# A transformer block written as one list of steps: the first loads, the order of the steps, and one core of a Trainium2

## The chip, the cores and the metric

One NeuronCore of one Trainium2 chip runs the kernel. The metric is device time in microseconds (us). The engines named here are TensorE (PE; its weight loads have a row of their own, PEld), VectorE (DVE), ScalarE (ACT), GpSimd (POOL) and SyncE (SP). DMAs are issued from SP and from ACT; in the profile such a row carries the name of the issuing queue, SPq or ACTq.

## The reference

```
x = A_x                                    # 2048 rows of 448, bf16
xn = layernorm(x)
q, k, v = split(xn @ wqkv)                 # 16 heads of 28
phi(a) = [softmax(a @ w_phi), softmax(-a @ w_phi)]      # per head, over 28 features
kv = phi(k)^T v ; z = sum of phi(k)
o = phi(q) kv / (phi(q) z + 1e-6)
out = x + o @ wo + mish(xn @ w1 + b1) @ w2               # w1 448 x 1792, w2 1792 x 448
```

## The kernel before

The 2048 rows are 16 tiles of 128 rows (t = 0 to 15), taken in 8 pairs (u = t // 2). For each tile the mean and the variance are found (on DVE, or on ACT in three steps at lines 493 to 497), then the reciprocal root (on ACT at lines 513 and 515, or on POOL at lines 508 and 510), then the normalised rows `xn`. Each pair is turned on its side into `xnT`, by TensorE with a copy behind it (pairs 0 and 1), or by a DMA that transposes (the others, line 551). Each row pair has 448 = 3 x 128 + 64 columns, so each product with a weight runs in three parts: A and B are the 128-row chunks, in two halves of the array that work side by side, and H is the last 64 rows.

The weights of the feature maps are folded: `Wpk` is the key weight times `w_phi`. TensorE first turns the key weights (`w_tr`, line 583; half 0 needs only the main part, rows 0 to 383, and half 1 needs the tail too, rows 384 to 447), then multiplies by `w_phi` (`w_mm`, line 613). The query weights come already turned, by four DMA transposes `lqT0` to `lqT3` (line 307); a copy on DVE (`qd`, line 311) doubles their last columns, and `w_mm` makes `Wpq`. Then come the products of keys, values and queries (line 464, `k`, `v`, `q`), exponentials on ACT (lines 720 and 793), the sums on DVE and the scaling of the keys on POOL (lines 728 to 744, `kn` and `kc`), the first matmul of the feed-forward part with its Mish on ACT (`f`, lines 464 and 814), `kv` (line 761), the attention (`nd`, line 834), its output projection (`wo`, line 956) and the second matmul of the feed-forward part (`g`, line 939), and the stores.

Every step is a small function that has a short name. A string `ORDER` lists the names, and `run_order` calls them one after the other, so each engine gets its instructions in the order of that list. Nothing else decides the order: semaphores are put in where a step reads what another engine or a DMA wrote. The names that matter here: `lx a.b` loads x tiles a to b-1, from SP (`s`) or ACT (`a`); `lkm` and `lvm` load the main part of the key and of the value weights, `lkt` and `lvt` their tails; `st` finds mean and variance, `rt` and `rs` the reciprocal root, `xn` normalises, `xt` turns a pair; `wtk0`, `wtk1` turn the key weights, `wmk` and `wmq` multiply by `w_phi`; `z` and `y` are matmuls on zeros that only keep TensorE running (line 405).

The tail of the key weights is one DMA of 64 rows by 896 columns, which also holds the tail of the value weights for the lower half of the array; the second tail load brings the value weights for the upper half:

```
def load_kv_tail(i, eng):
    lo, hi = HALF[i]
    dst, src = (Wv, A_wqkv[384:448, 2 * D:3 * D]) if i else (Wkv, A_wqkv[384:448, D:3 * D])
    dma(eng, lambda e: e.dma_start(dst[lo:hi, 3, :], src), w=[("Wt", i)], tag=f"ldWt{i}")
...
r = [("Wk", 0)] + ([("Wt", 0)] if h else []) + [("ident",)]          # w_tr: what half h reads
```

Of the kernel before, what the change touches and what calls it, by code (L numbers as in the profile page):

```python
# [144 lines left out]


ORDER = """
zero pw pp table lx0.2a lkma lx2.4s lkta lvta lbs st2d st1d lx4.6a pi st3a z11 st0d lps rt1a lvms rt3a rt2p xn1a xn2d
rt0p xn3d lx10.12s b1 xn0d wtk0b wtk1b xt1a lx8.10a xt0d lqT3 wmk0a st4d lqT2 st5d wmk1a v1Ba rt4p lqT1 xn4p lqT0 v0Ba
l1c0a v1Aa lx6.8s lx12.14s l1c1s v0Ha st10d v1Ha rt5p qd v0Aa st11d k1A k1H wmq1a st9d rt10p rt9p wmq0a rt11p k0B k1B  # L150
xn5d st8d k0A rt8p st7d xn10d q0A st12d xn11d xn8p xt2m k0H st6d st13d q0H xn9d q1B lx14.16s rs3p xn7d q0B xn6d q1A
rt12p st15d rt13p k2A xn12d xt5m k2H xn13d v2Ad q1H k2B q2B st14d xt4m v2Bd q2A k5A xt3m v2Hd rs7p xt6m q2H xn15p k5B
v5Ba k5H v4Aa v5Ha v4Ha xn14a kn2.0 k4H kn0.0 kc5 kn2.1 k4A v4Ba v5Aa k4B e2 k3B e3 xt7m v6Hd l1c2s v6Ad k3H q4H k3A
l1ts v6Bd e0 q4B kn0.1 k6B kn4.1 kn4.0 q4A pv k6H v7Bd k7H k6A k7B v7Hd los f0.8B v7Ad ep k7A f0.8H f0.6B f0.4B e5
f0.6A f0.8A f0.6H v3Ba f0.4A e8 v3Ha f0.7B v3Aa f0.1A kn1.0 f0.4H f0.7A f0.7H kc6 kn7.1 e1 f0.1H kn7.0 f0.3B f0.1B q7B
f0.3H kn1.1 f0.3A q5H kn3.1 e4 q3B q5B q3H e9 q3A q5A f1.4B kn3.0 q7H q7A f1.4A l2p1s kv0 kv7 e11 kv4 kv6 kv5 pk kv2
kv3 kv1 e14 f1.12B kvz f1.3B e10 f1.12A f1.4H wob f1.3A f1.3H f0.12B f1.12H f1.9A f1.9H f0.5H f0.5A f1.9B f0.0H f0.5B
f0.0B nd1 f0.0A f0.9A e15 f0.12H f0.9H f0.12A nd0 f0.10A e6 f0.9B f1.10B f0.10H f1.6A f1.6H nd2 l2p0a f0.10B f1.6B
l2p3s ot0m f1.10A f1.10H f1.1H f1.11B f1.1A f1.11H nd4 f1.1B f1.7B f1.11A e7 f1.8H nd3 f1.7A f1.8B f1.0H f1.0A ot1m
f1.7H f0.13H f0.13A f1.0B f1.5H f0.13B f1.8A f1.5B nd6 f0.2B f1.5A f0.2H f1.2H f0.2A f1.2A nd5 f1.13H f1.2B f1.13B  # L160
f0.11A l2p2a f0.11H nd7 q6A f1.13A q6H f0.11B ot2m q6B wo0H ot3m wo0A nd11 nd10 wo0B e12 g1 g7 e13 ot5m g0 wo3A nd12
nd13 wo2A wo2H wo3B ot6m wo2B nd14 wo3H g6 g5 g11 g4 g10 nd15 wo5B wo6A ot7m nd9 wo5A sto2 wo5H nd8 wo6B g12 g2 g8 g3
g14 ot4m wo1H wo4B wo1B wo7B wo4A wo1A wo6H wo4H wo7H wo7A sto0 g13 g9 sto1 stt14 g15 sto6 sto5 y0.1 sto3 sto4 y3.4
stt15
"""


# [942 lines left out]
```

## Time and profile before

| | |
|---|---|
| median of 3 runs | 155.65 us (150.18 to 155.79) |
| the profiled execution's own time | 150.82 us |
| its span in the trace | 149.0 us |
| PE busy | 145.1 us, 97% of the span |
| DVE, ACT, POOL busy | 99.3, 76.3, 43.2 us |
| DMA moved | 17.17 MB |

Times in the trace count from the span's start. A row gives start, duration, engine, line, operation, output <- input and how many instructions are merged in it; in square brackets stands how long the engine was idle before it and what ended that. A busy TensorE is not one at its peak, since matmuls overlap: the distance between starts tells more.

### The profile page before, as it was taken

The page shows a single profiled execution, that of the slowest core. Times are in us where ns is not written, and L with a number is a line of the kernel's source. Part 1 is how long each engine was busy: PE and PEld are TensorE (multiplying, and loading weights), DVE is VectorE, ACT ScalarE, POOL GpSimd, SP SyncE. Part 2 cuts the span into 40 slices and gives each one's busy share as a digit, 9 for nine tenths or more (in the row PEclk, how much of TensorE's full clock was granted, in tenths as well). Part 3 has the DMA queues.
Part 4 walks back from the last instruction along what each step waited for, and adds up shares of the span by engine and source line. Part 5 has one row for each costly group of instructions (what it writes and reads, how often), then busy time and mean ns, then how long its engine had stood idle before and what let it go on. Part 6 is the DMA issues. An engine that isn't in the chain of part 4 may idle for free.

```text
span 149.0 us, 3632 instructions
## 1 busy us (share of the span) xinstructions
PE 145.1 (97%) x1544; PEld 75.2 (50%) x1545; DVE 99.3 (67%) x222; ACT 76.3 (51%) x91; POOL 43.2 (29%) x66
## 2 busy tenths in 40 slices
PE   7897999999999999999999999999999999999996
PEld 2464544555444484454444545545555555547453
DVE  0885999999999303089794799588993399301722
ACT  3895999998988995774757839400000000000000
POOL 5425683999999992000000000000000000000000
DMA  4999459999997038974702133943030023220252
GB/s 121 320 249 317 106 132 164 157 239 218 212 224 183 4 57 107 191 168 122 133 4 40 26 92 66 109 93 62 7 62 0 0 41 87 56 67 4 92 185 92
DMA packets 40372, 17.17 MB, mean 115 GB/s; under 512 B 34084, under 2 KB 39844, under 8 KB 40356
## 3 DMA queue, kind: packets, MB, share of 16 engines
q1 hardware_dynamic: 38148, 14.37, 48.4%
q10 hardware_dynamic: 2208, 2.56, 5.8%
q8 instruction: 12, 0.20, 0.6%
q14 instruction: 4, 0.03, 0.1%
HBM read 6.97 MB, written 1.84 MB: 59 GB/s over the span
## 4 chain that ended last, share of the span: by engine, by line
PE 90%; SPq 5%; DMA 3%; issue 0%; DVE 0%
PE PS L464 48%; PE PS L939 28%; PE PS L956 7%; DMA WqT<-in_A_wqkv_dram 3%; SPq L307 2%; PE PS L834 2%; PE PS L761 2%; SPq L330 1%; PE PS L405 1%; PE PS L613 1%; SPq L287 1%; SPq L334 0%; SPq L290 0%; PE PS L921 0%; DVE WqT L311 0%
## 5 line engine op out<-in xcount | busy, mean ns | idle before, releaser
L464 PE MATMUL PS<-xnT,W 64*128 64x512 bf16 x392 | 45.3, 376 | 0.0
L939 PE MATMUL PS<-W,actT 128*128 128x448 bf16 (+1 forms) x224 | 42.7, 351 | 0.0
L814 ACT ACTIVATE actT<-PS,b1T 128x1024 bf16<-128x1024 f32 x28 | 30.1, 1112 | 12.2 <-PE PS L464 12.2
L939 PEld LDWEIGHTS PS<-W,actT 128*128 128x128 bf16 x224 | 21.6, 98 | 20.7 <-issue 1.3
L464 PEld LDWEIGHTS PS<-xnT,W 64*128 64x128 bf16 x392 | 18.1, 94 | 21.3 <-ACT actT L814 0.8
L904 DVE TENSOR_TENSOR x_all<-PS,x_all 128x448 bf16<-128x448 f32 (+1 forms) x16 | 9.3, 615 | 17.0 <-PE PS L956 9.2
L732 POOL TENSOR_TENSOR actT<-actT,rSk 128x896 bf16<-128x896 bf16 x12 | 20.0, 1697 | 0.0
L720 ACT ACTIVATE actT<-PS 128x896 bf16<-128x896 f32 x16 | 14.2, 1034 | 0.7 <-PE PS L464 0.7
L464 PE MATMUL PS<-Wpk,xnT 64*128 64x448 bf16 x112 | 13.2, 349 | 0.0
L464 PE MATMUL PS<-Wkv,xnT 64*128 64x448 bf16 x112 | 13.1, 349 | 0.1
L464 PE MATMUL PS<-Wpq,xnT 64*128 64x448 bf16 x112 | 13.0, 349 | 0.0
L728 DVE TENSOR_REDUCE Sk<-actT 128x32 f32<-128x896 bf16 x12 | 12.5, 1040 | 0.0
L849 DVE COPY Sq<-PS 128x16 f32<-128x16 f32 x32 | 4.0, 168 | 12.1 <-PE PS L834 12.1
L501 DVE BATCH_NORM_STATS2 stats<-x_all 128x6 f32<-128x448 bf16 x15 | 9.2, 610 | 4.1 <-DMA x_all<-in_A_x_dram 4.1
L860 DVE TENSOR_TENSOR xn<-v_all,rden 128x448 bf16<-128x448 f32 x16 | 10.0, 624 | 2.2 <-DMA Wkv<-xn 1.7
L857 DVE TENSOR_TENSOR v_all<-v_all 128x464 f32<-128x464 f32 x16 | 10.3, 643 | 0.6
L853 DVE TENSOR_TENSOR v_all<-PS,Sq 128x464 f32<-128x464 f32 x16 | 10.3, 641 | 0.5
L855 DVE TENSOR_TENSOR v_all<-PS,Sq 128x464 f32<-128x464 f32 x16 | 10.1, 630 | 0.0
L793 ACT ACTIVATE actT<-PS 128x896 bf16<-128x896 f32 x10 | 8.8, 987 | 0.3 <-PE PS L464 0.3
L464 PEld LDWEIGHTS PS<-Wkv,xnT 64*128 64x128 bf16 x112 | 5.3, 94 | 5.5 <-ACT actT L720 0.3
L464 PEld LDWEIGHTS PS<-Wpq,xnT 64*128 64x128 bf16 x112 | 5.3, 94 | 5.3 <-ACT Eq L793 0.3
L464 PEld LDWEIGHTS PS<-Wpk,xnT 64*128 64x128 bf16 x112 | 5.4, 94 | 5.1 <-ACT actT L793 0.4
(84 smaller groups left out, 135.5 us busy)
## 6 DMA issues: line engine op xcount, KB each, us to landing
out_dram<-x_all SPq DMA_DIRECT2D x7, 224.0 KB, 2.2
W<-in_B_w_dram SPq DMA_DIRECT2D x3, 448.0 KB, 4.9
x_all<-in_A_x_dram SPq DMA_DIRECT2D x5, 224.0 KB, 4.4
W<-in_B_w_dram ACTq DMA_DIRECT2D x2, 448.0 KB, 3.8
x_all<-in_A_x_dram ACTq DMA_DIRECT2D x3, 224.0 KB, 3.8
Wo<-in_A_wo_dram SPq DMA_DIRECT2D x2, 336.0 KB, 5.3
W<-in_B_w_dram SPq DMA_DIRECT2D x2, 224.0 KB, 4.9
Wkv<-in_A_wqkv_dram ACTq DMA_DIRECT2D x1, 336.0 KB, 4.4
```

Source lines behind the costliest of these rows:

```text
L464: ins = e.matmul(o, lhs(c, k), rhs(c, k), start=first and n == at[par][0], stop=last and n == at[par][-1])
L720: op("ACT", lambda e, s=s: e.activation(E_of(u)[:, s, :, :], two(b, D), ACT.Exp, scale=1.0 if s == 0 else -1.0), r=[pb(b), pb(b + 1)], w=[ ...
L728: op("DVE", lambda e: e.tensor_reduce(Sk[u][:, s, :], Eh(), AX.X, ALU.add), r=[("E", u, s)], w=[("Sk", u, s)], tag=f"Sk{u}.{s}")
L732: op("POOL", lambda e: e.tensor_tensor(Eh(), Eh(), ap_on(rSk[u][:, s, 0:1], [[1, 2 * H], [0, DH]]), ALU.mult), r=[("E", u, s), ("rSk", u, ...
L814: op("ACT", lambda e: e.activation(actT[:, q, fc, :], bank(b, 2), ACT.Mish, bias=b1T[:, fc:fc + 1]), r=[("b1T",), pb(b), pb(b + 1)], w=[(" ...
L853: op("DVE", lambda e: e.tensor_tensor(tv(t1[i]), num(0), sx(1), ALU.mult), r=[pb(b), pb(b + 1), ("Sq", i, 1)], w=[("t1", i)], tag=f"ta{t}")
L855: op("DVE", lambda e: e.tensor_tensor(tv(t2), num(1), sx(0), ALU.mult), r=[pb(b), pb(b + 1), ("Sq", i, 0)], w=[("t2",)], tag=f"tb{t}")
L857: op("DVE", lambda e: e.tensor_tensor(t1[i], t1[i], t2, ALU.add), r=[("t1", i), ("t2",)], w=[("t1", i)], tag=f"tc{t}")
L860: op("DVE", lambda e: e.tensor_tensor(o_sb[(t // 2) % 2][:, t % 2, :].rearrange("p (h d) -> p h d", d=DH), t1[i][:, :, 0:DH], ap_on(rden[i ...
L904: op("DVE", lambda e: e.tensor_tensor(x_all[:, t, 0:n], bank(b)[:, 0:n], x_all[:, t, 0:n], ALU.add), r=[pb(b), ("x", t)], w=[("out", t)], ...
L939: ins = e.matmul(bank(b)[:, 0:width(t)], act_of(fc, t), W2[:, fc, 0:width(t)], start=first and fc == 0, stop=last and fc == FC - 1)
L956: ins = e.matmul(bank(b)[:, 0:w], oT_of(u)[lo:hi, cc * P:(cc + 1) * P], Wo[lo:hi, cc, 0:w], start=first and n == at[par][0], stop=last and ...
```

## The change

Only the list `ORDER` changes; no step's function does. What the words for it mean in the list: the first x loads become `lx1.2s`, `lx2.4a`, `lx0.1a` (tile 1 alone from SP, tiles 2 and 3 from ACT, tile 0 alone from ACT) in place of `lx0.2a` and `lx2.4s`; the key weights' main part comes from SP (`lkms`) and both tails follow on ACT, behind ACT's statistics of tile 3 (`lkta`) and behind the reciprocal root of tile 2 (`lvta`); the third part of W2 (`l2p2a`) is loaded early; the values of pair 1 begin with part H; and the rest of the list stands in another order, with another choice of engine for some copies, roots and normalisations.

```
-zero pw pp table lx0.2a lkma lx2.4s lkta lvta lbs st2d st1d lx4.6a pi st3a z11 st0d lps rt1a lvms rt3a rt2p xn1a xn2d
-rt0p xn3d lx10.12s b1 xn0d wtk0b wtk1b xt1a lx8.10a xt0d lqT3 wmk0a st4d lqT2 st5d wmk1a v1Ba rt4p lqT1 xn4p lqT0 v0Ba
-l1c0a v1Aa lx6.8s lx12.14s l1c1s v0Ha st10d v1Ha rt5p qd v0Aa st11d k1A k1H wmq1a st9d rt10p rt9p wmq0a rt11p k0B k1B
...
-g14 ot4m wo1H wo4B wo1B wo7B wo4A wo1A wo6H wo4H wo7H wo7A sto0 g13 g9 sto1 stt14 g15 sto6 sto5 y0.1 sto3 sto4 y3.4
-stt15
+lx1.2s zero st1d lx2.4a pi pw lbs st2d lx0.1a table lkms st0d st3a lkta y0.1 rt1p rt2a lvta xn1d y1.2 z7 lps xn2d rt3a
+rt0a lx8.12s lvms lx4.6s b1 xn3d lqT0 xn0d lqT3 wtk0b wtk1b xt1a st10d lqT2 xt0b wmk0a st11d lqT1 wmk1a st9d lx6.8s pp
+rs5a v1Ha st5d v1Aa v0Ba st4d l2p2a qd v1Ba rs2p v0Aa st8d v0Ha lx12.14a rt9a rt8p k1H k0H xn5d xn4d xn11d k1A l1c1s
+xn8d st6d xn10d rt6p wmq1a wmq0a k0B k1B xn9p lx14.16s st7d q0H st14d k0A st12d q1H st15d rt7p q0B q1B xt2m xt5m q0A
...
+g3 g9 ot4m sto0 wo4B wo7B wo6H wo6A wo1B wo4H wo4A wo1A wo1H wo7A wo7H wo6B sto5 g8 g13 sto2 g12 sto1 sto4 g14 sto6
+g15 stt14 stt15
```

On ACT, at the program's start, before the change: all of its first five DMAs stand ahead of the first statistics (line 493, tile 3). Line 287 loads x, line 290 the main part of the key weights, line 304 the two tails.

```order
L351 ACT_TABLE_LOAD
L287 DMA x_all<-in_A_x_dram 128x896
L290 DMA Wkv<-in_A_wqkv_dram 128x3x448
L304 DMA Wkv<-in_A_wqkv_dram 64x896
L304 DMA Wkv<-in_A_wqkv_dram 64x448
L287 DMA x_all<-in_A_x_dram 128x896
L493 ACTIVATE junk1,mv<-x_all 128x448 [waits dma_0]
```

And with the change, at the same place on ACT (dma_58 is the load of tiles 2 and 3):

```order
L287 DMA x_all<-in_A_x_dram 128x896
L287 DMA x_all<-in_A_x_dram 128x448
L351 ACT_TABLE_LOAD
L493 ACTIVATE junk1,mv<-x_all 128x448 [waits dma_58]
L495 ACTIVATE rmean<-mv 128x1 [waits done_ACT]
L497 ACTIVATE junk1,mv<-x_all,rmean 128x448 [waits done_ACT]
L304 DMA Wkv<-in_A_wqkv_dram 64x896
L513 ACTIVATE lnv<-mv,eps_col 128x1 [waits done_POOL,done_DVE]
L515 ACTIVATE rstd<-lnv 128x1 [waits done_ACT]
L304 DMA Wkv<-in_A_wqkv_dram 64x448
```

The two tails (line 304) moved behind three and behind five instructions of ACT that each have a wait, and the main part of the key weights left this queue.

On SP, at the start, before the change; line 334 loads b1, line 330 the four pieces of `w_phi`, line 290 the main part of the value weights, line 307 the transposes of the query weights:

```order
L287 DMA x_all<-in_A_x_dram 128x896
L334 DMA b1_rows<-in_B_b1_dram 14x128
L330 DMA Wbd<-in_A_w_phi_dram 28x4x28 [waits done_POOL]
L330 DMA Wbd<-in_A_w_phi_dram 28x4x28 x3
L290 DMA Wkv<-in_A_wqkv_dram 128x3x448
L287 DMA x_all<-in_A_x_dram 128x896
L307 DMA_TRANSPOSE WqT<-in_A_wqkv_dram 128x448 x4
```

And with the change; the first line 290 is now the key weights, the second the value weights:

```order
L287 DMA x_all<-in_A_x_dram 128x448
L334 DMA b1_rows<-in_B_b1_dram 14x128
L290 DMA Wkv<-in_A_wqkv_dram 128x3x448
L330 DMA Wbd<-in_A_w_phi_dram 28x4x28 [waits done_POOL]
L330 DMA Wbd<-in_A_w_phi_dram 28x4x28 x3
L287 DMA x_all<-in_A_x_dram 128x1792
L290 DMA Wkv<-in_A_wqkv_dram 128x3x448
L287 DMA x_all<-in_A_x_dram 128x896
L307 DMA_TRANSPOSE WqT<-in_A_wqkv_dram 128x448 x4
```

The four transposes of the query weights moved behind two more issues.

On PE, the first products behind the zero matmuls, with the change (dma_2 is the main part of the key weights, dma_60 the first tail, dma_61 the second); before the change the same rows stand there in the same order up to the first line 464, with 11 zero matmuls in place of 10:

```order
L405 MATMUL PS<-zeros 128x512 [waits done_POOL]
L405 MATMUL PS<-zeros 128x512 x9
L806 MATMUL PS<-ident,b1_rows 128x14 [waits dma_1,done_POOL]
L583 MATMUL PS<-ident,Wkv 112x128 [waits dma_2]
L583 MATMUL PS<-ident,Wkv 112x128 x7
L583 MATMUL PS<-ident,Wkv 112x128 [waits dma_60]
L583 MATMUL PS<-ident,Wkv 112x128 x3
L583 MATMUL PS<-ident,Wkv 112x64 x4
L539 MATMUL PS<-ident,xn1 128x128 [waits done_DVE]
L539 MATMUL PS<-ident,xn1 128x128 x6
L539 MATMUL PS<-ident,xn0 128x128 [waits done_DVE]
```

Nothing moved here: the second half of the key weights' turn (the row that waits dma_60) still stands ahead of the turn of the first rows (line 539) and of all that follows.

More of the change, by code (lines that the diff above doesn't have):

```diff
@@ L147 @@
 ORDER = """
-zero pw pp table lx0.2a lkma lx2.4s lkta lvta lbs st2d st1d lx4.6a pi st3a z11 st0d lps rt1a lvms rt3a rt2p xn1a xn2d
-rt0p xn3d lx10.12s b1 xn0d wtk0b wtk1b xt1a lx8.10a xt0d lqT3 wmk0a st4d lqT2 st5d wmk1a v1Ba rt4p lqT1 xn4p lqT0 v0Ba
-l1c0a v1Aa lx6.8s lx12.14s l1c1s v0Ha st10d v1Ha rt5p qd v0Aa st11d k1A k1H wmq1a st9d rt10p rt9p wmq0a rt11p k0B k1B
-xn5d st8d k0A rt8p st7d xn10d q0A st12d xn11d xn8p xt2m k0H st6d st13d q0H xn9d q1B lx14.16s rs3p xn7d q0B xn6d q1A
-rt12p st15d rt13p k2A xn12d xt5m k2H xn13d v2Ad q1H k2B q2B st14d xt4m v2Bd q2A k5A xt3m v2Hd rs7p xt6m q2H xn15p k5B
@@ L153 @@
[L153 to L162, printed above, removed]
@@ new lines @@
+xn6d q1A v2Bd k2A v2Hd xt4m st13d pv rt14a rt12p l1c0a xn7d v2Ad k2H k5B rt13p rt15p k2B xn13d k5A v5Ad pk xt3m k5H
+xn12d k4H k4A xn14p v5Bd xt6m v4Ha e2 k4B v4Aa e3 kn2.1 xn15p kn1.1 v5Hd q2B v4Ba q2H q2A k3B q4B v6Bd xt7m l1c2a
+kn4.0 k3A kn4.1 e4 v6Hd l1ta k6A kn1.0 k3H k6H v6Ad q4H k6B q4A v3Bd k7A k7H kn2.0 kn3.0 v3Ad v3Hd e9 e0 k7B f0.4B
+f0.3A f0.4H e5 v7Ha e1 f0.3B f0.4A kc0 f0.1B v7Ba f0.3H f0.7B f0.1A f0.1H loa e8 f0.8A f0.7H f0.7A f0.8B v7Aa q3A
+l2p1a f0.6B q3H f0.8H kn7.1 f0.6A ep f0.6H f1.4A q3B q7B q5A l2p0s kn6.0 kn6.1 kn3.1 f1.4B q5B q7A q7H q5H kv1 kv2 kv4
@@ new lines @@
+kv6 kv3 kc5 kv5 kv0 kn7.0 kv7 e15 kvz f1.4H f1.3H f1.1B f1.3A f1.11A e10 f1.1H f1.11H e14 f1.3B f1.9B f1.11B f1.9A
+f1.9H f0.5H f1.1A f0.10A f0.10H f1.0A f1.0H nd3 l2p3a f0.10B f0.5A f1.0B f0.5B nd0 f1.6B f1.12H f1.12A f1.2H f1.6H
+f1.6A f1.2B f1.12B nd1 f0.2B f1.2A e7 f0.2A f1.5H f0.2H f1.7A nd2 f1.7H f1.5B e11 f0.13H f1.7B f0.13A ot0m f1.5A nd4
+e6 ot1m f1.8B f0.13B f1.8H f1.8A f0.9A nd6 f1.13B f1.10H f0.9H f1.13H f1.13A f1.10B nd7 f1.10A f0.11B f0.9B f0.0B
+f0.11H nd5 f0.11A f0.12B f0.0A f0.12A f0.0H q6A f0.12H ot3m q6H ot2m wo0B nd11 wo0A q6B e12 wo0H nd10 g0 g1 g6 e13
@@ L165 @@
+nd13 wob ot5m wo3A wo3H nd12 ot6m wo3B nd14 g11 g7 g10 nd8 wo2B wo5H wo5A wo2A sto3 nd15 wo2H nd9 wo5B ot7m g4 g5 g2
+g3 g9 ot4m sto0 wo4B wo7B wo6H wo6A wo1B wo4H wo4A wo1A wo1H wo7A wo7H wo6B sto5 g8 g13 sto2 g12 sto1 sto4 g14 sto6
+g15 stt14 stt15
 """
```

## The prediction

> **What bounds the kernel now.** I read the page's busy table first, then the chain that ended last, then the timeline of its start.
>
> ```profile
> PE 145.1 (97%) x1544; PEld 75.2 (50%) x1545; DVE 99.3 (67%) x222; ACT 76.3 (51%) x91; POOL 43.2 (29%) x66
> ```
>
> ```profile
> 8.56 5.07 DMA WqT<-in_A_wqkv_dram
> ...
> 13.65 0.24 DVE WqT L311
> ...
> 13.94 0.96 PE PS L613 x16
> 14.90 37.59 PE PS L464 x382
> 52.49 3.27 PE PS L761 x128
> ...
> 146.11 0.41 PE PS L921 x14
> ```
>
> From 14.90 us to 146.52 us the chain is TensorE alone, 131.6 us without a break. The work in that stretch is the same before and after. 382 matmuls in 37.59 us are 0.098 us each. So the time is the moment at which this dense stretch begins, plus what TensorE must still do, plus a tail of 149.0 - 146.5 = 2.5 us for the last addition and store, which the change leaves (tile 15 is still last and still split). The zero matmuls that stood at the very end run beside that store and give nothing back.
>
> What ends last ahead of the stretch is the DMA transpose of the query weights, which lands at 13.63; the product that reads it starts at 13.94. What TensorE does earlier is in the timeline:
>
> ```profile
> 0.96 4.68 PE L405 MATMUL PS<-zeros 128*128 128x512 bf16 x11 [0.96 <-POOL zeros L357]
> 1.28 0.46 ACTq L290 DMA_DIRECT2D Wkv<-in_A_wqkv_dram  x1
> 1.78 1.17 ACTq L304 DMA_DIRECT2D Wkv<-in_A_wqkv_dram  x2
> 4.13 0.58 ACT L493 ACTIVATE junk<-x_all 128x448 bf16<-128x448 bf16 x1 [2.03 <-DMA x_all<-in_A_x_dram]
> 5.07 0.67 ACT L497 ACTIVATE junk<-x_all,rmean 128x448 bf16<-128x448 bf16 x1
> 5.71 1.31 PE L583 MATMUL PS<-ident,Wkv 128*112 128x128 bf16 x16
> 7.43 1.22 PE L539 MATMUL PS<-ident,xn 128*128 128x128 bf16 x14 [0.42 <-DVE xn L527]
> 8.04 0.33 ACTq L287 DMA_DIRECT2D x_all<-in_A_x_dram  x1
> 8.06 0.58 ACT L544 ACTIVATE Eq<-PS 112x512 bf16<-112x512 bf16 x1
> 8.54 0.91 ACT L544 ACTIVATE xnT<-PS 128x896 bf16<-128x896 bf16 x1
> 9.51 2.82 PE L464 MATMUL PS<-Wkv,xnT 64*128 64x448 bf16 x28
> 12.16 0.92 PE L464 MATMUL PS<-Wpk,xnT 64*128 64x448 bf16 x8
> 13.94 0.96 PE L613 MATMUL PS<-Wbd,WqT 112*128 112x112 bf16 x16 [0.85 <-DVE WqT L311]
> ```
>
> The last row is the only wait of any size behind 9.51: 0.85 us. The gain that a better start could bring is therefore small: this wait, and some of the gaps ahead of 9.51.
>
> **The change, part by part.** The first load's size. Tiles 2 and 3 go out first on ACT, at about 0.85 us, and ACT's statistics of tile 3 (4.13 above, behind a load of the same size issued at 0.81) stay where they were, at 4.15. Tile 1 alone is half the bytes; its saving is bounded by the store rows:
>
> ```profile
> out_dram<-x_all SPq DMA_DIRECT2D x7, 224.0 KB, 2.2
> out_dram<-x_all SPq DMA_DIRECT2D x1, 112.0 KB, 1.7
> Wkv<-in_A_wqkv_dram ACTq DMA_DIRECT2D x1, 336.0 KB, 4.4
> Wkv<-in_A_wqkv_dram SPq DMA_DIRECT2D x1, 336.0 KB, 4.7
> Wkv<-in_A_wqkv_dram ACTq DMA_DIRECT2D x1, 112.0 KB, 4.4
> ```
>
> At most 0.5 us earlier for `xn1`, which nothing can use while TensorE waits for weights. I take 0.
>
> The key weights' main part. It moves from 1.28 on ACT to 1.27 + 0.44 + 0.05 = 1.76 on SP; with 4.4 us to landing it is there at 6.16 and not at 5.68. TensorE turns its first half at 6.2, half a microsecond late. What hides this is the next part.
>
> The tails. This is the term that I expect to decide. A DMA on ACT's queue is issued when the waits of the instructions ahead of it are met, not when ACT has run them: the row of 8.04 goes out before the copies of 8.06 and 8.54 that stand ahead of it have started. By the order, the first tail now stands behind the three steps of tile 3's statistics; the wait of the last (the row of 5.07) is met at about 5.06. So the tail is issued at **5.1 us** and not at 1.78. Queued behind it on ACT is nothing that another engine waits for sooner. Its time to landing: 4.4 us by its own row, where it stood behind 560 KB on the same queue; the x loads go from 2.7 to 5.0:
>
> ```profile
> DMA to landing us min/median/max: 2.7/3.9/5.0
> ```
>
> I take the median, 3.9, since its queue is now empty but SP's holds 784 KB: it lands at **9.0 us** (7.8 to 10.1). TensorE takes its instructions in order, and the second half of the key weights' turn stands ahead of everything else. So TensorE is idle from about 6.7 to 9.0.
>
> From there to the values: eight transposes 0.45 us, seven of pair 1 0.4 us, 0.2 us until the last has landed; beside it ACT copies the turned weights (0.58 us, the row of 8.06, done at 10.2), then the turned pair 1 (0.91 us), and the values start at 9.0 + 2.2 = **11.2** against 9.51. The second tail goes out behind tile 2's root, at 6.15 (that row stood at 6.13 before), and lands by 10.6 with the 4.4 us: in time. Then 28 + 10 matmuls of 0.098 us, as the order has two more key products ahead of the query weights: TensorE is at the query weights' product at 11.2 + 3.72 = **14.9** (13.7 to 16.0 with the landing).
>
> The query weights. These rows give what the transposes stand behind on SP:
>
> ```profile
> 0.81 0.40 SPq L287 DMA_DIRECT2D x_all<-in_A_x_dram  x1
> 1.27 0.44 SPq L334 DMA_DIRECT2D b_rows<-in_B_b_dram  x1
> 1.76 1.92 SPq L330 DMA_DIRECT2D Wbd<-in_A_w_phi_dram  x4
> 3.73 0.42 SPq L290 DMA_DIRECT2D Wkv<-in_A_wqkv_dram  x1
> 4.19 0.48 SPq L287 DMA_DIRECT2D x_all<-in_A_x_dram  x1
> 4.71 5.12 SPq L307 DMA_TRANSPOSE WqT<-in_A_wqkv_dram  x4
> ```
>
> Two more issues, 0.46 and 0.52 us, put the first at 5.69 and the fourth at 9.54. With the 5.07 us of the chain it lands at 14.61; the copy (0.24) and 0.05 + 0.05 us put the product at **14.95**. With the shortest of the four times to landing, 4.1, it would be 14.0. Both paths meet at 14.95, which is 1.01 later than 13.94, with two more matmuls (0.2 us) done: **+0.8 us**. The third part of W2, issued on ACT behind ACT's next wait (11 us or later), shares the DMA engines with the last transpose; that is within the 5.07, which had a 448 KB load of W1 beside it.
>
> The new order of the rest. TensorE has 131.6 us of work either way; its cover is that each next operand is there. The nearest thing to a limit is POOL, which scales the keys:
>
> ```profile
> 26.15 1.04 POOL L533 TENSOR_SCALAR xn<-x_all,rstd,shift 128x64 bf16<-128x64 bf16 x2 [0.94 <-DMA xnT<-xn]
> 27.16 3.35 POOL L732 TENSOR_TENSOR actT<-actT,rSk 128x896 bf16<-128x896 bf16 x2
> 46.31 8.32 POOL L732 TENSOR_TENSOR actT<-actT,rSk 128x896 bf16<-128x896 bf16 x5
> ```
>
> Before, the last scaling ends at 54.6, 0.3 us ahead of the `kv` that reads it (seventh of eight, 52.49 + 6 x 0.41 = 54.95). Now tile 14 is normalised on POOL too (0.7 us), and waits as tile 15 did for the transpose of pair 3; with that landing at about 27.1, 1 us later than before, 16 scalings of 1.67 us and the two normalisations end at 55.6, and the last `kv` stands at 53.3 + 7 x 0.41 = 56.2. Slack 0.6 us: I take 0. The far ends: +1.4, that transpose 2 us later still; and -1.4, the two longest waits of TensorE's weight loads in the stretch all gone, though matmuls ran beside them, so that little of it is there to gain:
>
> ```profile
> PEld PS L464 <- ACT actT L814: 0.8, 3, 0.3
> PEld PS L464 <- DVE v_all L855: 0.6, 2, 0.3
> ```
>
> Sum against the profiled execution: 150.82 + 0.8 = **151.6 us**. That execution is 0.64 us above the lowest run shown, 150.18, and 4.83 below the median, 155.65, a level of which this trace shows nothing. From 2% a measurement of this kernel tells a change from none: below 147.8 or above 153.8 by the profiled execution.
>
> **The rivals.**
>
> The tail is no wait: were it issued early or landed by 8 us, the landing of the query weights alone would set the product, at 14.0 to 14.9, less the 0.2. Time 150.7 to 151.6, or 149.3 with the whole -1.4. For it speaks the emptier queue; against it that the issue needs the wait of the row of 5.07.
>
> TensorE's rate falls back. The zero matmuls at the start take 4.68 / 11 = 0.43 us each for 512 columns, where this stretch at the end has four in 1.04:
>
> ```profile
> 146.57 1.04 PE L405 MATMUL PS<-zeros 128*128 128x512 bf16 x4
> ```
>
> So TensorE starts at half its rate and has the full one only after 4.3 to 4.8 us of running. With the change the zero matmuls end at 0.96 + 10 x 0.43 = 5.2, and until 9.0 only one group of eight transposes (0.45 us) runs. If this gap takes the rate back, the next 4.3 us of running, from 9.0 on, count half: +2.15 us, 153.8; if twice as long, +4.3, 155.9. It decides from the point where the gap is long enough, and ends on the slow side. For it: 3.4 us idle of 3.8. Against it: nothing in this trace shows a fall. The Trainium skill, "TensorE: Matmul & The Clock Gate", in "What's actually happening", has the clock halved after a free-running window of about 3.4 us without activity, and restored after a busy one; by that rule the gap is about as long as one window, so it would hit some executions and spare others. No run here shows it yet.
>
> The feed. POOL's scalings or the late transposes come 1 to 2 us later than I have them: the `kv` products wait, 152.6 to 153.6. For it: slack of 0.6 us. Against: pairs 2 to 6 are turned, by the same hand count, about 1 us before TensorE reads them.
>
> The two levels. If what lifts two of the three runs to 155.7 lies in this start, the change may end it or fix it: 151.6 would then stand 2.6% under 155.65, or 155.65 + 0.8 = 156.5 over it. Nothing speaks for either.
>
> **How the numbers follow.** Forecast 151.6 (own range 150.8 to 152.6): 0.47. Tail no wait: 0.17. Rate falls back: 0.17. Feed: 0.07. Levels: 0.12, mostly upward in time. The range leaves out the far ends of the first two rivals and takes in the levels: 149.8 to 156.9. Faster by over 2% comes only from the levels, 0.10, as no sum from the rows reaches 147.8. Slower by over 2%: the rate's fall, and a little of the feed and the levels, 0.20. Within 2%: 0.70.
>
> **What would show it.** Right: a line 493 of ACT at 4.1, the first line 304 on ACTq at 5.1, the second eight of line 583 on PE behind an idle time of over 2 us that ends at about 9.0, the values (line 464) from 11.2, the product of the query weights (line 613) from about 15, and from there about 131.4 us to the last line 921. Wrong: an idle time under 0.5 us ahead of the second half of line 583 (tail no wait); 28 value matmuls in 5 us and not 2.8 (rate); idle POOL ahead of line 732 and idle PE ahead of line 761 (feed).

## Result, and the profile after

The changed kernel takes 160.83 us (median of 6 runs, 159.4 to 161.27). Against the kernel before, timed on the same chip, the ratio is **1.067, 95% interval 1.058 to 1.076**: slower by 6 to 8%. The forecast was 151.6 us, with a range up to 156.9. The profiled execution takes 160.7 us with a span of 159.0 us, 10.0 us longer than before. (The kernel before reads 150.0 to 150.7 us as a median on the chips of the experiments; runs more than 1.5% above the fastest of their kernel are left out of all ratios.)

On the page after, the row of TensorE's busy share (40 slices of 4.0 us) has a hole in the second and third slice and another in the eleventh; the row of the granted clock (PEclk, in tenths) shows 5 in the third and fourth, and 8 and 7 in the eleventh and twelfth:

```profile
PE   7539999999399999999999999999999999999993
...
PEclk9955999999879999999999999999999999999999
```

The timeline of the start, with the rows that answer to those of the prediction:

```profile
4.77 0.53 ACTq L304 DMA_DIRECT2D Wkv<-in_A_wqkv_dram  x1
...
5.72 0.65 PE L583 MATMUL PS<-ident,Wkv 128*112 128x128 bf16 x8 [0.29 <-DMA Wkv<-in_A_wqkv_dram]
...
10.60 1.18 PE L583 MATMUL PS<-ident,Wkv 128*112 128x128 bf16 x8 [4.23 <-DMA Wkv<-in_A_wqkv_dram]
...
14.82 3.05 PE L464 MATMUL PS<-Wkv,xnT 64*128 64x448 bf16 x28
...
18.75 0.96 PE L613 MATMUL PS<-Wbd,WqT 112*128 112x112 bf16 x16
```

The tail goes out at 4.77 as foreseen, TensorE is idle for 4.23 us until it has landed, and the product of the query weights starts at 18.75 and not at 13.94. From there to the end of the last line 921 are 137.8 us (156.53), where it was 132.6 before; behind it both kernels have 2.5 us. So of the 10.0 us the **start has 4.8** and the **dense stretch 5.2**. Where the stretch loses is seen in the list of TensorE's waits, and in the chain:

```profile
PE PS L583 <- DMA Wkv<-in_A_wqkv_dram: 4.5, 2, 4.2
PE PS L464 <- DMA xnT<-xn: 2.7, 1, 2.7
```

```profile
4.77 5.79 DMA Wkv<-in_A_wqkv_dram
...
34.32 7.83 DMA xnT<-xn
...
42.29 12.19 PE PS L464 x98
```

The second wait is for the DMA transpose of pair 7, which takes 7.83 us. What stands on the queues around it, after, and then around the same transpose before (the row at 28.47):

```profile
33.78 0.34 ACTq L294 DMA_DIRECT2D W<-in_B_w_dram  x1
34.16 0.47 ACTq L298 DMA_DIRECT2D W<-in_B_w_dram  x1
34.32 1.31 SPq L551 DMA_TRANSPOSE xnT<-xn  x1
35.01 0.48 ACTq L298 DMA_DIRECT2D W<-in_B_w_dram  x1
```

```profile
28.47 1.26 SPq L551 DMA_TRANSPOSE xnT<-xn  x1
29.78 0.69 SPq L294 DMA_DIRECT2D W<-in_B_w_dram  x1
30.51 1.19 SPq L298 DMA_DIRECT2D W<-in_B_w_dram  x2
```

Before, the third block of W1 and its last rows (448 and twice 224 KB) stand on SP, behind the transpose, which took 3.3 us. After, they are issued from ACT, two of them just ahead of the transpose and one 0.7 us behind it.

The third cost is the clock. Busy time, granted clock and DMA share of core 0 in stretches, after:

```profile
8.00:9.00 1.00, 0.00 (x0) 0.74 1.00 281
9.00:12.00 3.00, 1.40 (x11) 0.50 1.37 150
12.00:15.00 3.00, 3.00 (x32) 0.50 0.93 245
15.00:16.00 1.00, 1.00 (x10) 0.84 0.73 283
...
42.00:43.00 1.00, 0.71 (x6) 0.81 0.22 45
43.00:46.00 3.00, 3.00 (x18) 0.50 0.95 178
46.00:47.00 1.00, 1.00 (x12) 0.98 2.48 133
```

The means of the mixed rows give the edges (a mean of 0.74 over 8 to 9 is full clock up to 8.48 and half behind it): at half from about 8.5 to 15.3, and again from about 42.6 to 46.0. The first fall comes in the middle of the wait, the second when work has been going for 0.3 us already. These lengths are twice 3.4 us and once 3.4 us, and the 27.3 us from the end of the one to the start of the other are eight times 3.4: the edges lie on one grid. One such window at half takes 0.5 x 3.41 / 155 = 0.011 off the mean clock of an execution, so the mean clock counts them: this one has 0.967, three windows, and all six executions have 0.967 or 0.968.

The Trainium skill, "TensorE: Matmul & The Clock Gate", section "What's actually happening", gives a free-running window of 3413 ns; the lengths here agree.

### The profile page after: what moved, and what is told of

It is laid out like the page before. It is cut to its first block, busy times and chain, and to the rows that moved or that the text cites. A ratio compares the mean times of both kernels' runs of the same rounds, so it can differ in the third digit from the quotient of the medians.

```text
span 159.0 us, 3626 instructions
## 1 busy us (share of the span) xinstructions
PE 148.2 (93%) x1539; PEld 79.9 (50%) x1539; DVE 100.3 (63%) x223; ACT 76.8 (48%) x96; POOL 40.5 (25%) x59
## 4 chain that ended last, share of the span: by engine, by line
PE 76%; DMA 10%; ACT 8%; POOL 2%; DVE 1%; issue 1%; ACTq 0%
PE PS L464 35%; PE PS L939 27%; PE PS L956 7%; DMA xnT<-xn 5%; DMA Wkv<-in_A_wqkv_dram 4%; ACT actT L720 3%; PE PS L834 2%; PE PS L761 2%; DMA x_all<-in_A_x_dram 2%; PE PS L613 1%; ACT Wpq L544 1%; POOL actT L732 1%; ACT actT L793 1%; ACT Eq L793 1%; PE PS L539 1%; PE PS L583 1%
## 5 line engine op out<-in xcount | busy, mean ns | idle before, releaser
L464 PEld LDWEIGHTS PS<-xnT,W 64*128 64x128 bf16 x392 | 19.6, 94 | 20.6 <-issue 2.0
L464 PE MATMUL PS<-Wpk,xnT 64*128 64x448 bf16 x112 | 13.8, 370 | 2.7 <-DMA xnT<-xn 2.7
L720 ACT ACTIVATE actT<-PS 128x896 bf16<-128x896 f32 x16 | 13.4, 939 | 5.9 <-DVE v_all L546 4.4
L464 PE MATMUL PS<-Wkv,xnT 64*128 64x448 bf16 x112 | 14.3, 371 | 0.0
L464 PEld LDWEIGHTS PS<-Wkv,xnT 64*128 64x128 bf16 x112 | 5.9, 99 | 6.1 <-issue 1.2
L793 ACT ACTIVATE actT<-PS 128x896 bf16<-128x896 f32 x10 | 8.7, 968 | 0.0
```

Source lines behind the costliest of these rows:

```text
L464: ins = e.matmul(o, lhs(c, k), rhs(c, k), start=first and n == at[par][0], stop=last and n == at[par][-1])
L720: op("ACT", lambda e, s=s: e.activation(E_of(u)[:, s, :, :], two(b, D), ACT.Exp, scale=1.0 if s == 0 else -1.0), r=[pb(b), pb(b + 1)], w=[ ...
L793: op("ACT", lambda e, s=s: e.activation(Eq_of(u)[:, :, s, :].rearrange("p i (h n) -> p i h n", n=64)[:, :, :, 0:QP], two(b, D).rearrange(" ...
```

## Experiments

The theory formed from the two traces has three mechanisms: the late tail with the clock that falls in its wait, the transpose slowed by W1's loads, and small things in the rest of the order. The rival is that the new order as a whole feeds TensorE worse. Every edit is one of the list alone; a line with - and + shows it, relative to the kernel named.

**The tails early** (in the kernel after):

```
-... lx0.1a table ... st3a lkta y0.1 rt1p rt2a lvta xn1d ...
+... lx0.1a lkta lvta table ... st3a y0.1 rt1p rt2a xn1d ...
```

> The changed kernel (160.7 us) with both tails of the key and value weights issued on ACT at once behind the x loads, ahead of the table and of tile 3's statistics; the key weights' main part stays on SP. Theory (the late first tail costs 4.2 us of idle TensorE and then half the clock until 15.7): the second eight of line 583 start by 6.7, the clock stays at 1.00 in the start, the query weights' product is at about 14.9 (its own transposes) and not at 18.75: about 156.5 us. Rival (the start is bound by the query weights' transposes behind two more issues on SP, or by the x loads): product still at 17 or later, 159 us or more.

Measured: 156.38 us (155.42 to 160.09), ratio 1.040 [1.034, 1.047]. The slowest of the four runs is the profiled one. In it the key weights' main part is what the turn waits for, until 6.82, with the tail there, and the product starts at 14.85, right behind the matmuls ahead of it; the query weights' copy was done at 13.60. But pair 7's transpose is worse than ever, and TensorE waits 6.2 us for it:

```profile
30.62 11.15 DMA xnT<-xn
41.91 11.98 PE PS L464 x98
```

It takes 11.15 us, with the same three loads of W1 on ACT beside it (from 29.88); why more than the 7.83 after isn't settled, and it is the figure of the slowest run alone. The start is mended by 3.9 us, and the second mechanism stands by itself.

**W1 behind the transpose** (in the kernel after):

```
-l1c2a, l1ta where they stand; ... v6Bd xt7m ...
+... v6Bd xt7m l1c2s l1ts ...
```

> The changed kernel with the third row block of W1 and its two tails issued from SP right behind the transpose of pair 7, not from ACT beside it. Theory (these 896 KB share the DMA engines with that transpose, which lands after 7.8 us where six others took 2.9 to 5.4, and TensorE waits 2.9 us for it and loses the clock for 3.3 us): the transpose lands in under 4.5 us, no idle TensorE at 39 to 42, no second fall of the clock: about 156 us. Rival (the transpose is late because POOL's normalisation of tile 15 stands behind a scaling): idle TensorE stays over 1.5 us, 159 us or more.

Measured: 157.53 us (156.71 to 158.03), ratio 1.050 [1.046, 1.054]. TensorE no longer waits for a transpose at all, though in the profiled run the start is worse than after by about 1 us:

```profile
11.18 1.18 PE L583 MATMUL PS<-ident,Wkv 128*112 128x128 bf16 x8 [4.24 <-DMA Wkv<-in_A_wqkv_dram]
```

The clock is 0.978 in all four runs: two windows at half, those of the start. The third window went with the wait.

**Both edits**:

> The changed kernel with both edits, tails early and W1 behind the transpose. If the two losses are separate and are all of it: 160.7 - 4.0 - 4.7 = 152 us, near the fast runs of the kernel before. If something else in the new order costs as well: 153.5 us or more.

Measured: 153.17 us (152.99 to 154.4), ratio 1.024 [1.019, 1.029]. The two edits take 2.7 and 1.8% off the 6.7, together 4.3: they add. The start still has one window at half in three of the four runs (clock 0.989); in the profiled one the main part comes at 7.15 from SP, behind the first x load and beside the tails, and TensorE waits 2.1 us for it. The fourth run has a clock of 1.0 and is the slowest, at 154.4, which is not explained.

**Zero matmuls in the wait** (in the kernel after, the late tail kept):

```
-wtk0b wtk1b
+wtk0b z16 wtk1b
```

> The changed kernel with 16 more matmuls on zeros between the two halves of the key weights' turn, so that TensorE runs while it waits for the tail. Clock theory: the clock stays at 1.00 up to the tail's landing at 10.6, the values start 2.2 us behind it, at 12.8 and not at 14.8, and the time falls by about 2 us to 158.6, though TensorE waits as long for the tail as in the changed kernel. Rival (the clock is no cause, the 4.2 us from the tail to the values are the copies on ACT and DVE): values still at 14.5 to 15, 160.7 us.

Measured: 159.45 us (157.37 to 160.23), ratio 1.054 [1.048, 1.060]. In the profiled run the clock is 1.00 throughout:

```profile
6.34 3.66 PE L405 MATMUL PS<-zeros 128*128 128x512 bf16 x16
...
11.08 0.75 PE L583 MATMUL PS<-ident,Wkv 128*112 128x128 bf16 x8 [1.08 <-DMA Wkv<-in_A_wqkv_dram]
...
17.14 1.14 PE L613 MATMUL PS<-Wbd,WqT 112*128 112x112 bf16 x16
```

The landing is as late as ever, but the same eight matmuls take 0.75 us and not 1.18, and from there to the product are 6.06 us where the kernel after needs 8.15. So the fall of the clock at the start costs about **2.1 us**, apart from the wait itself. In two of the four runs one window still fell (0.988 and 0.989). The profiled run is 3.5 us shorter than the median after, as the later fall is missing in it too, though TensorE waits 2.3 us for pair 7's transpose.

**Only the late tails, in the kernel before**:

```
-lkta lvta lbs ... st3a z11 ... rt3a rt2p
+lbs ... st3a lkta z11 ... rt3a lvta rt2p
```

> The kernel before (150.0 us) with one edit: the two tails moved on ACT behind tile 3's statistics and behind its root, as the change has them; the key weights' main part stays on ACT. Theory (issue behind the statistics is enough): the first tail goes out at about 5.1, lands after 4 to 6 us at 9 to 11, TensorE idles 2.5 to 4.5 us ahead of the second half of line 583, the clock falls to half, the query weights' product comes at 16.5 to 18.5 and not at 13.9: 153 to 155 us. Rival (the late landing needs the key weights on SP and the other loads of the change): landing under 4 us, 151 us.

Measured: 154.07 us (153.26 to 154.91), ratio 1.027 [1.021, 1.032].

```profile
5.08 4.35 DMA Wkv<-in_A_wqkv_dram
...
17.82 37.59 PE PS L464 x382
...
149.03 0.41 PE PS L921 x14
```

The tail lands at 9.43, near my forecast of 9.0. The dense stretch is then the same to 0.01 us (37.59), and all of the 2.9 us (149.03 against 146.11) come from the start: the tail's place alone makes the kernel slower by over 2%, with one or two windows at half in each run.

**Less on SP** (in the kernel after, the load of tiles 8 to 11 behind `lqT3`):

> The changed kernel with the 448 KB load of tiles 8 to 11 issued behind the second transpose of the query weights, so that SP's queue holds 336 and not 784 KB ahead of the tail. If the tail's 5.8 us come from sharing the DMA engines with SP's loads: it lands in 4.8 us or less, TensorE's idle time falls by 1 us or more and the time to about 159. If they come from the transposes or from the tail's own shape (64 rows on half of the partitions): 5.5 us or more, 160.7.

Measured: 158.46 us (2 runs), ratio 1.056 [1.051, 1.061].

```profile
9.64 1.18 PE L583 MATMUL PS<-ident,Wkv 128*112 128x128 bf16 x8 [3.08 <-DMA Wkv<-in_A_wqkv_dram]
```

With 448 KB less on the other queue the tail takes 4.65 us, against 5.79, 5.99 and 6.17 in the three profiles with the start of after. The landing depends on what both queues carry, as the Trainium skill has it in "DMA: Bandwidth & Descriptors", section "Issuing engines are not separate DMA queues": DMAs from different issuing engines share the same 16 DMA engines and interleave. This run agrees.

The time does not show this gain, though. The product is at 18.71, as late as after: the clock fell 0.9 us later, and was at half until 16.2. The 2.3 us by which the profiled span is shorter come from the dense stretch, where TensorE waits 2.1 us for pair 7's transpose and the clock does not fall (0.978, two windows). The windows of this run have edges at 9.4 and 16.2; in steps of 3.41 us from there, that wait lies across the edge at 40.1, with 0.6 us in one window and 1.5 in the next, which is still 55% busy.

**The start of the loads of before, and W1 behind the transpose** (in the kernel after: `lx0.2a lkma lx2.4s lkta lvta`, tiles 4 and 5 on ACT, the value weights ahead of tiles 8 to 11, eight zero matmuls for seven):

> The changed kernel with W1 behind the transpose of pair 7 and with the whole start of the loads as before the change (x in pairs of tiles, the main part of the key weights on ACT, tails right behind it, 11 zero matmuls); all that follows in the new order. If the two losses are all and the rest of the new order is neutral: 149.5 to 150.5 us, no fall of the clock. If the rest of the order costs by itself: 151 or more, and TensorE's dense stretch is longer than 131.6 us.

Measured: 152.26 us (151.93 to 152.96), ratio 1.015 [1.011, 1.019]. The product is at 13.82, no later than before, but the stretch from there to the last line 921 takes 134.1 us and not 132.6: the rest of the new order costs by itself, about 1.5 us.

**Both edits, and nine more zero matmuls ahead of the main part**:

> The kernel with both edits of e3_both (153.2 us; TensorE idle from 5.3 to 7.2, clock at half from about 8 to 11) and 19 zero matmuls at the start in place of 10, so that TensorE runs on until the key weights land. Clock theory: the clock stays at 1.00, the values start about 1.4 us sooner: 151.5 to 152 us; what is then left over the kernel before is the later landing of the key weights, 7.2 for 5.7. Rival (the clock costs nothing there): 153.2.

Measured: 152.76 us (152.57 to 153.17), ratio 1.018 [1.014, 1.022], clock 1.000 in all four runs. The zeros last until 8.05, the product is at 14.60 and not at 15.22 as with both edits alone. So the clock is held, but the theory's 1.4 us are not there: the zeros run on past 7.15, when the main part had landed in the run without them, and the time is 0.4 us lower, with overlapping intervals.

**Wo's loads from SP** (in the kernel with the start of before, `loa` becomes `los`). The profile had shown the four issues on ACT ahead of a Mish copy (line 814); with the start of before, and then with Wo on SP:

```profile
43.62 2.26 ACTq L348 DMA_DIRECT2D Wo<-in_A_wo_dram  x4
45.93 1.11 ACT L814 ACTIVATE actT<-PS,b1T 128x1024 bf16<-128x1024 f32 x1 [1.20 <-PE PS L464]
47.19 0.82 PE L464 MATMUL PS<-xnT,W 64*128 64x512 bf16 x6 [0.32 <-ACT actT L814]
```

```profile
44.53 2.32 SPq L348 DMA_DIRECT2D Wo<-in_A_wo_dram  x4
45.26 1.11 ACT L814 ACTIVATE actT<-PS,b1T 128x1024 bf16<-128x1024 f32 x1 [0.40 <-PE PS L464]
```

> The kernel after, with the start of loads of the kernel before and W1's third block behind pair 7's transpose (152.26 us when it ran without the edit of this run), and here with the four loads of Wo on SP, where the kernel before has them, in place of ACT. Theory: on ACT the four issues of 2.1 to 2.7 us hold up the Mish copy behind them, and TensorE waits for it; without them the time falls by about 1 us, to 151.2, and the row of line 814 that waited 1.1 to 1.2 us for PE does not stand behind four issues. Rival: what is left of the difference to before lies in the late transposes and the rest of the order; then 152.0 to 152.5.

Measured: 151.87 us (151.31 to 153.19), ratio 1.011 [1.007, 1.015]. The mechanism is there, the copy starts with the matmuls before it and TensorE's 0.32 us are gone, but that is a third of the price I gave it, and the interval overlaps that of the run without the edit, so the times do not show the gain. My theory's 151.2 falls; what is left of 1% lies elsewhere. In the trace, the stretch from the product to the last line 921 is 1.3 us longer than before (13.90 to 147.74): 0.5 us is a wait for pair 6's transpose, and 0.8 us no wait of TensorE names. That transpose took 6.57 us, and a block of W1 had gone out on ACT 0.8 us ahead of it (23.11 against 23.87): the picture of pair 7 again, but no run moved this load. TensorE's weight loads do wait more for ACT's exponentials than before (1.2 us in 4 places against 0.3 in one):

```profile
PEld PS L464 <- ACT actT L720: 1.2, 4, 0.4
```

That this is the 0.8 us was not tried.

**Only W1 on ACT, in the kernel before** (`l1c2a l1ta` ahead of `k4B`, in place of `l1c2s l1ts` on SP):

> The kernel before with only W1's third block and its tails moved from SP, where they go out behind pair 7's transpose, to ACT, where they go out beside it. Theory (a transposing DMA is slowed by plain loads on the other queue): pair 7's transpose takes over 6 us from issue to landing in place of 3.3, TensorE waits for it by 0 to 2 us, time 150.0 to 152. Rival (the long landing in the kernel after comes from its own place or from the load of the x tiles): it lands in under 4.5 us and the time stays at 150.0.

Measured: 152.14 us (151.42 to 152.63), ratio 1.010 [1.005, 1.016].

```profile
27.43 0.33 ACTq L294 DMA_DIRECT2D W<-in_B_w_dram  x1
27.44 1.43 SPq L551 DMA_TRANSPOSE xnT<-xn  x1
27.79 0.51 ACTq L298 DMA_DIRECT2D W<-in_B_w_dram  x1
28.34 0.62 ACTq L298 DMA_DIRECT2D W<-in_B_w_dram  x1
...
34.14 0.74 PE L464 MATMUL PS<-Wkv,xnT 64*128 64x448 bf16 x6 [1.46 <-DMA xnT<-xn]
```

The transpose now takes 6.56 us and not 3.3, and TensorE waits 1.46 us: the second mechanism is shown by itself, in another order of the work. Over all the profiles of this case, pair 7's transpose took 2.9 to 3.3 us in the twelve with these loads behind it on SP, and 6.6 to 11.2 us in the five with them on ACT. The clock stays at 1.0 in all four runs.

This trace shows one thing more. Up to the product of the query weights its list is that of the kernel before, and yet:

```profile
11.95 0.23 DVE L311 COPY WqT<-WqT 128x256 bf16<-128x256 bf16 x1
...
13.00 0.96 PE L613 MATMUL PS<-Wbd,WqT 112*128 112x112 bf16 x16
```

The product follows the matmuls ahead of it without a wait, 0.94 us sooner than in the profiled execution of before. The wait of 0.85 us for the query weights, with which the prediction begins, is not in every execution of this start.

**The query weights first, in the kernel before**:

```
-lvta lbs ... rt1a lvms rt3a ... xn3d lx10.12s b1 ... lqT0 v0Ba
+lvta lvma lbs ... rt1a rt3a ... xn3d b1 ... lqT0 lx10.12s v0Ba
```

> The kernel before with the four transposes of the query weights directly behind the four pieces of w_phi on SP, the load of x tiles 10 and 11 behind them, and the value weights' main part on ACT behind the two tails. The transposes then go out about 0.9 us sooner. Theory (the query weights' landing sets the start of the dense stretch): the product of the query weights at about 13.1 us in place of 13.94, time 149.2 against 150.0. Rival (the transposes share the DMA engines with the value weights and land no sooner, or the x tiles come late): 150.0 or above.

Measured: 153.95 us (153.51 to 155.29), ratio 1.024 [1.018, 1.029]: the theory missed, and what the rival named last happened. Tiles 10 and 11, behind the transposes, come too late, and DVE has the statistics of tile 10 (line 501) ahead of the copy that the product waits for (line 311):

```profile
13.79 0.63 DVE L501 BATCH_NORM_STATS2 stats<-x_all 128x6 f32<-128x448 bf16 x1 [2.74 <-DMA x_all<-in_A_x_dram]
14.63 0.23 DVE L311 COPY WqT<-WqT 128x256 bf16<-128x256 bf16 x1
...
14.91 0.96 PE L613 MATMUL PS<-Wbd,WqT 112*128 112x112 bf16 x16 [1.89 <-DVE WqT L311]
```

A wait of 1.89 us is enough for the clock here. All six runs have 0.989, and the rows of the profiled one show the fall behind the wait, at 15.98, when TensorE has worked for 1.1 us again; the 3.4 us ahead of it, from 12.57, were 45% busy:

```profile
14.00:15.00 1.00, 0.09 (x2) 1.00 0.98 385
15.00:16.00 1.00, 1.00 (x18) 0.99 0.46 174
16.00:17.00 1.00, 1.00 (x8) 0.50 0.19 63
```

**The same with two zero matmuls** behind the turn of the key weights:

> As the run with the query weights first, with two zero matmuls behind the turn of the key weights, where TensorE waits for the first rows. Theory (TensorE's clock falls after a window with little work, and this start is near it): the same time, 149.2 to 149.5, and nothing lost for the 0.4 to 0.9 us of zero matmuls, since they stand in a wait. Rival (they push the values back): 0.4 us more than the run without them.

Measured: 151.79 us (150.81 to 153.94), ratio 1.008 [1.004, 1.012]; 4 of 12 runs at 0.989. In the profiled run tile 10 landed in 3.05 us, not 4.88, and the product was at 13.07 as foreseen, though that is no sooner than the 13.00 which the run above has with the loads of before. And pair 2's transpose, behind the same statistics, made TensorE wait 1.14 us at 19.63. The time is above the 149.5 of the theory, and above the kernel before.

**The value weights on ACT, and zero matmuls**, three kernels. First, zero matmuls alone in the two waits of before (`z2` behind `wtk1b`, `z3` ahead of `wmq1a`):

> The kernel before with two zero matmuls behind the turn of the key weights, where TensorE waits 0.42 us for the first rows, and three ahead of the product of the query weights, where it waits 0.85 us. Theory (the executions of before at 153 to 156 us are those in which TensorE's clock fell at the start, a granted clock of 0.989 or 0.978 in 5 of its 39 runs beside my experiments): no run under a clock of 0.99, and the median where before's undisturbed runs are, 149.9 to 150.5. Rival (the falls do not come from these waits): about one run in seven at a clock of 0.989 or below, as without the edit.

Measured: 150.63 us (150.47 to 151.25), ratio 1.003 [1.000, 1.006]. In its profile the query weights' copy starts at 12.08, so here too the second wait was not there to be filled. Then `lvma` behind `lvta` on ACT in place of `lvms` on SP, with `z2` in both waits, and then without zeros:

> The kernel before with the value weights' main part on ACT behind the two tails, so that the transposes of the query weights go out 0.46 us sooner, with the x tiles 10 and 11 still ahead of them, and with two zero matmuls at each of the two waits. Theory (the landing of the query weights sets the start, and the x tiles must stay ahead): product of the query weights at 13.5 in place of 13.94, time 149.5 against 150.0, no run at a clock under 0.99. Rival (the transposes are slowed as the value weights' load runs beside them on the other queue): product at 13.9 or later, 150.0 or above.

> As the run with the value weights on ACT, without the zero matmuls. Theory: 149.5 in most runs, with some at a lower clock as in the kernel before. Rival: 150.0 or above.

Measured: 150.38 us (150.26 to 151.42), ratio 1.003 [1.000, 1.006], and 150.08 us (149.79 to 151.0), ratio 0.999 [0.997, 1.002]. None of the three is clearly under the 150.1 us that the kernel before has as its median on this chip. The last one's profile:

```profile
11.80 0.23 DVE L311 COPY WqT<-WqT 128x256 bf16<-128x256 bf16 x1
...
12.96 0.96 PE L613 MATMUL PS<-Wbd,WqT 112*128 112x112 bf16 x16
...
18.98 0.93 PE L464 MATMUL PS<-Wpk,xnT 64*128 64x448 bf16 x8 [0.60 <-DMA xnT<-xn]
```

The product is at 12.96, 1.0 us sooner than in the profiled execution of before and sooner even than the 13.5 foreseen, but no more than the 13.00 without the edit. So no gain of the edit is shown at this place, and in most executions there was probably little to gain: two traces with the loads of before lack the wait, and before's profiled execution, at 150.82, lies 0.7 us above that median. What TensorE does wait for here is pair 2's transpose, 0.60 us. On the low clock, beside these three the kernel before had 5 of 29 runs at 0.989 or below, and the three 0 of 36. The median of all runs hardly differs, 150.08 against 150.1. As the version without zeros is free of it too, the zeros are not shown to be the reason; with 12 runs of each, that each one is free of it isn't certain either.

## Why the prediction was wrong

**Right**: the place of the tail's issue (4.77 for 5.1); that TensorE waits for the tail; that the dense stretch behind an unchanged feed keeps its length (37.59 us again in the kernel before with late tails); the equal end. The query weights, whose path I had at 14.95, set the product in neither trace: after, it stands at 18.75 behind a copy done at 17.0, and with the tails early, at 14.85 behind one done at 13.60. That 14.85 and 14.95 are so close is luck.

**The landing, 3.9 us.** This term was mis-sized: 5.79 us, beyond the range of 2.7 to 5.0 from which I took the median. I held the empty queue of ACT for an advantage. The run with less on SP shows that the other queue's bytes count: 4.65 us with 448 KB less. Cost at the start: 1.6 us (10.6 against 9.0).

**"Rate falls back", the rival at 0.17.** My sum took it at nothing, and it happened in every run of the kernel after (0.967 or 0.968 in all six), in the profiled one from about 8.5 us on. Its price there, 2.15 us by the rows, was right: the way from the tail to the product took 8.15 us against 5.9 forecast, and the run with zeros shows 2.1 us. The length behind that price was not: I had 4.3 us at half, and it was 6.8 us, of which TensorE worked in 4.7, so that the two prices come so close is luck. The step that failed is the chance. I wrote that nothing in the trace shows a fall, but a trace whose longest wait is 0.85 us can't show one, and my own sum had 3.4 us idle of 3.8. The start's 4.8 us (1.0 forecast, 1.6 from the landing, 2.2 from the clock) alone would give 155.6, inside the range. The Trainium skill, "TensorE: Matmul & The Clock Gate", section "What's actually happening", makes an idle window of about 3.4 us the condition of a fall. In the run with the query weights first a window with 1.5 of its 3.4 us busy fell as well, so the measurement goes beyond that sentence.

**"The new order of the rest", taken at 0.** This failed, with 5.2 us, beyond its bounds of -1.4 to +1.4. The hand count went over pairs 2 to 6 and left pair 7 out, and my bounds were built on POOL and on one transpose 2 us late. What the list did at that place, W1's third block from SP behind the transpose to ACT beside it, I did not see, as I had compared the issues on the queues at the start alone. The wait was 2.7 us, and it brought a third window at half speed, worth 1.7 us by an estimate (half of its 3.4 us). The runs with W1 moved show it both ways: out of the kernel after, 1.8%; into the kernel before, 1.0%. The other 0.8 us have no cause shown; the last repaired version also has 0.8 us that no wait of TensorE names, but that they are the same was not tried.

**The feed (POOL)** played no part: no wait for `kv` stands among TensorE's.

**The two levels.** Executions of before at 153 to 156 us mostly have a mean clock of 0.989 or 0.978, that is one or two windows at half, as the changed kernel has three in every run. But those at 0.989 are 3.8 to 5.0 us longer than 150.0, and one window at half is worth 1.7 us at most, so most of their difference must be waits. Which wait starts it in the kernel before isn't settled: none of those executions was profiled. Some of its runs at 152 to 153 us have a clock of 1.0 and are not explained by it.

## What to carry to other kernels

When a list of steps is reordered, compare for every DMA that TensorE waits for what is in flight beside it on all queues, not only what stands ahead of it on its own; and do it for the whole program. Beside the price of a TensorE wait of about 2 us or more, give a fall of the clock behind it a real chance, at up to 1.7 us for each window at half, even if the trace of before shows none: waits of 1.89 and 2.7 us brought one here, waits of 2.1 and 2.3 us did not. And before a plan rests on a wait that one trace shows, look whether a second execution has it: the 0.85 us for the query weights stood in one trace and were missing in two others with the same loads.

## What the hardware showed that was not expected

- A transpose by DMA of one pair, pair 7's, took 2.9 to 3.3 us with 896 KB of plain loads behind it on its own queue (12 profiles), and 6.56 to 7.83 us, once 11.15 us, with the same loads issued beside it from the other queue (5 profiles). A plain load spreads less: the tail, issued at about 5 us, took 4.35 to 6.17 us in the five profiles that have it late.
- The clock falls at the end of a window of 3.4 us, wherever the work stands then: in the middle of the long wait (8.5, in a wait from 6.4 to 10.6), or 0.3 us (42.6 against 42.3) and 1.1 us (16.0 against 14.9) into the work that follows a shorter one. It comes back 3.4 us later or, when the next window is half empty too (8.5 to 11.9, 1.3 us busy), 6.8 us later.
- The fall is not a matter of a gap as long as the window: a wait of 1.89 us within 3.4 us sufficed in all of six runs, with the window 45% busy. A wait of 2.1 us that lay across an edge brought none, with the emptier window 55% busy.
